# Converting the second network's weights during the first, storing them in DRAM, and reading its back-projection weights from there

## The chip, the cores and the metric

One core of a Trainium2 chip. The metric is device time of one launch in microseconds. The kernel before took 1028.5 us in the median of three runs (1026.12 to 1029.22).

## The reference, cut to what matters

The weights of both networks are float64 and reach the chip as such. Attention runs first (a full softmax over means of four rows, plus a local softmax over a band of seven positions); its output is x, 2304 tokens by 512. Two networks follow:

```
h = x @ w_in                 # 512 -> 2048
x = (h * cos(h)) @ w_out     # 2048 -> 512
a = x @ w_a                  # 512 -> 1536
b = x @ w_b
y = (a * b) @ w_out2         # 1536 -> 512
```

## The kernel before, in words

**Precision.** Each float32 operand of a matmul is split into a high part (rounded by a copy to fp32r on ACT) and a low part (a subtraction); a product is three matmuls, high times high, high times low and low times high (`mm3`, L417 to L421). A float64 weight of 128 x 512 arrives as pairs of 32-bit words (512 KB, tile `raw`) and is converted to float32 by one ACT instruction (L104) and two DVE instructions (L105, L106): this is one *conversion*.

**First network.** Tokens are cut into units of 288 (five) and 432 (two). A step g does one block of 128 hidden columns: `h_mm` (12 matmuls), cosine on ACT and DVE (`cos_a`, `cos_b`, L457 to L466), split into gh and gl (L470, L474), and three steps later `back_mm` (12 matmuls) into four accumulators. There are 112 steps; units 0 and 1 are done in two halves of 8 blocks each, so that their first half goes to `y_part` in DRAM and the second to `y_dram`. The attention of later units is dealt out over the steps by `unit_slots`, up to step 96. The 32 weight tiles of this network, as high and low parts, stay in SBUF in the pool `wp` (33 slots of 4 KB per partition).

**Second network.** It works on three groups G of 768 tokens, as a 2 x 2 block product with seven multiplications in place of eight (P1 to P7, over sums and differences of weight blocks and of x blocks). For each of six column blocks p and for a and b there are seven products (`product`, 6 matmuls each), written out by hand in the list `items` with the back-projection blocks (`back2`, 6 matmuls each) between them. Each group ends with a run of 24 back-projection blocks (its half h = 1) without products between. `load_x` fetches x from DRAM (and adds `y_part` on POOL for the tokens that have one, L630), `prep_x` forms the differences and splits seven x blocks (`xsplit`, L642, L643); both are done for the next group during that run, on DVE.

**Weights of the second network.** `take2` converts its 36 raw tiles and forms the sums of weight blocks on POOL (L593 to L596). It is called in the last 16 steps of the first network and during the products of the first group. `stage` (L717 to L726) then makes, a few items ahead, the high and low part of each weight block that an item needs, products and back-projection alike: a copy on ACT (L724) and a subtraction on POOL, every third on DVE (L726). Each group does this anew.

**Order.** A list scheduler sets the order on each engine from the program's order, the dependencies and the tiles' slots; each engine and SP's DMA queue then work strictly in that order. `after` adds an edge to this scheduling without a wait on the chip. SP issues all DMAs.

Of the kernel before, what the change touches and what calls it, by code (L numbers as in the profile page):

```python
# [9 lines left out]
F32 = mybir.dt.float32  # L10
# [13 lines left out]
KC = DM // 128  # L24
# [17 lines left out]
C = {'AHEAD': 8, 'LEAD': 4, 'NPRE': 4, 'ND': 'ddd', 'XL': 'dpp', 'SUMS0': 'dddd', 'SUMS1': 'pppp', 'GLO': 8, 'FS': 8, 'S1': 0.7, 'G2': 14, 'LC': 0, 'DM': 2, 'LAG': 3, 'NGS': 3, 'MK': 0, 'SB': 'ddd', 'NL': 'dpp', 'W0': 0, 'W1': 0, 'W2': 0, 'W3': 0, 'NWV': 3, 'NGH': 4, 'XB': 8, 'YE': 6, 'CA': 2, 'CV': 1.3, 'SA': 5, 'SD': 3, 'PA': 1, 'LAG2': 2, 'PK': 1.0, 'GE': 'ad', 'NXF': 3, 'LP': 0, 'T': {'sums': [0, 0.5, 1.0, 3.0], 'ls': [0, 0, 0, 1.5], 'ds': [1, 1.5, 3, 4], 'ex': 6, 'ln': [6.0, 9.5], 'dn': [6, 7, 9, 10], 'dt': [7, 9.5, 11, 12], 'lt': [7.5, 8.5, 12.0, 13.5], 'at': [9.5, 9.5, 13.5, 14.5], 'xh': [11.0, 12.0, 15.0, 15.5], 'xl': [12.5, 13.5, 15.5, 15.5]}, 'T1': {'sums': [0, 0, 1.0, 2.0], 'ls': [0.5, 1.5, 2.5, 3.5], 'ds': [1, 1.5, 3, 4], 'ex': 5, 'ln': [5.5, 8], 'dn': [5.0, 6.0, 8.0, 9.0], 'dt': [6.0, 7.5, 10.0, 11.0], 'lt': [7.0, 8.0, 12.0, 12.0], 'at': [9, 9, 13, 14], 'xh': [9.0, 10.0, 13.0, 14.0], 'xl': [9.5, 11, 15, 15]}}  # L42
# [16 lines left out]
def kernel(ctx, tc, qT, kT, vw, vds, w_in, w_out, w_a, w_b, w_out2, out):  # L59
# [42 lines left out]
    def to_f32(raw, out=None):  # L102
        lw, hh = raw[:, :, 0], raw[:, :, 1]
        act.activation(out=hh.bitcast(F32), in_=hh.bitcast(F32), func=AF.Prelu, scale=2.0 ** -112, alpha=2.0 ** 32)  # L104
        dve.tensor_scalar(out=lw, in0=lw, scalar1=29, scalar2=None, op0=ALU.logical_shift_right)  # L105
# [90 lines left out]
    def local_scores(u, hp):  # L196
# [21 lines left out]
        mx = at.tile([128, NW], F32, tag="mx", name="mx", bufs=3)  # L218
# [21 lines left out]
    def exps(u):  # L240
# [5 lines left out]
        for hp in range(HP if u < C["DM"] else 0):  # L246
            sm = smd[u, hp]
            sdr[u, hp] = at.tile([QD, 2], F32, tag="sd", name="sd", bufs=3)
# [247 lines left out]
    if True:  # L496
# [61 lines left out]
        order2 = [(nm, p + NP * i) for p in range(NP) for nm in "ab2" for i in range(2)]  # L558
        raw2, w1, w2, ssl = {}, {}, {}, {}
        cv = [0, 0]  # L560

        def fetch2(upto):
            while cv[0] < min(upto, len(order2)):
                nm, f = order2[cv[0]]
                raw2[nm, f], _ = wload(srcs[nm][f])
                cv[0] += 1

        def sblock(nm, p, k):
# [3 lines left out]
            return ssl[b // 4][:, b % 4]  # L572

        def take2(upto):
            while cv[1] < min(upto, len(order2)):
                nm, f = order2[cv[1]]
                i, p = divmod(f, NP)
                dst = w2 if nm == "2" else w1
                if (nm, p) == ("2", NP - 1):
                    fetch2(cv[1] + (3 if cv[1] < 30 else 2))  # L580
                    r = raw2.pop((nm, f))
                    to_f32(r)
                    w2[nm, p, i] = r[:, :, 0].bitcast(F32)
                    cv[1] += 1
                    continue
                if i == 0:
                    dst[nm, p] = wp.tile([128, 4, 256], F32, tag="w", name="w1", bufs=33)
# [285 lines left out]
```

## Time and profile before

| | us |
|---|---|
| profiled execution | 1030.88 |
| its span | 1029.1 |
| PE busy | 968.1 (94%) |
| DVE busy | 748.9 (73%) |
| ACT busy | 592.1 (58%) |
| POOL busy | 398.6 (39%) |

The busy share of PE in 40 equal slices of the span, each digit a tenth (9 is 90% or more), with that of DVE below:

```profile
PE   5978899999999899999979899999799999999998
DVE  7889966685757465663598998877877778686773
```

A slice is 25.7 us. The first network's steps end near 600 us, the groups of the second end near 742, 886 and 1026 us. Matmuls are pipelined, so that the busy time of PE is no measure of its pace; the number of matmuls in a stretch is.

### The profile page before, as it was taken

The page shows a single profiled execution, that of the slowest core. Times are in us where ns is not written, and L with a number is a line of the kernel's source. Part 1 is how long each engine was busy: PE and PEld are TensorE (multiplying, and loading weights), DVE is VectorE, ACT ScalarE, POOL GpSimd, SP SyncE. Part 2 cuts the span into 40 slices and gives each one's busy share as a digit, 9 for nine tenths or more (in the row PEclk, how much of TensorE's full clock was granted, in tenths as well). Part 3 has the DMA queues.
Part 4 walks back from the last instruction along what each step waited for, and adds up shares of the span by engine and source line. Part 5 has one row for each costly group of instructions (what it writes and reads, how often), then busy time and mean ns, then how long its engine had stood idle before and what let it go on. Part 6 is the DMA issues. An engine that isn't in the chain of part 4 may idle for free. (4 is left out here: it accounts for less than half of the span.)

```text
span 1029.1 us, 18838 instructions
## 1 busy us (share of the span) xinstructions
PE 968.1 (94%) x6936; PEld 920.2 (89%) x6936; DVE 748.9 (73%) x1524; ACT 592.1 (58%) x1390; POOL 398.6 (39%) x499
## 2 busy tenths in 40 slices
PE   5978899999999899999979899999799999999998
PEld 4767789999999799899878799999799999999998
DVE  7889966685757465663598998877877778686773
ACT  4677666474757456565656654545544446544453
POOL 4878731002100300000174484446644444544452
PEclk9989899999999999999999999999899999999999
DMA  9645421211120210000463640002200002000000
GB/s 301 216 160 205 123 73 38 77 48 55 58 69 20 82 31 27 29 2 1 119 223 123 235 149 1 1 1 86 76 9 1 2 1 93 32 1 1 2 32 31
DMA packets 35035, 72.84 MB, mean 71 GB/s; under 512 B 3968, under 2 KB 19840, under 8 KB 34944
## 3 DMA queue, kind: packets, MB, share of 16 engines
q1 hardware_dynamic: 34944, 71.65, 21.7%
q8 instruction: 55, 0.90, 0.4%
q14 instruction: 36, 0.29, 0.1%
HBM read 61.01 MB, written 10.62 MB: 70 GB/s over the span
## 5 line engine op out<-in xcount | busy, mean ns | idle before, releaser
L726 POOL TENSOR_TENSOR sb<-w,sb 128x256 fp32r<-128x256 f32 x183 | 144.4, 791 | 265.7 <-ACT sb L724 241.9
L744 DVE TENSOR_TENSOR ev<-ev,z 128x384 f32<-128x384 f32 x252 | 134.9, 549 | 56.4 <-PE z L420 50.3
L724 ACT ACTIVATE sb<-w 128x256 fp32r<-128x256 f32 x264 | 109.2, 416 | 95.7 <-PE z L420 70.3
L418 PE MATMUL h<-xh,w 128*128 128x288 f32 (+1 forms) x448 | 147.4, 329 | 13.8 <-DVE gs L466 13.6
L418 PE MATMUL acc<-gh,w 128*128 128x288 f32 (+1 forms) x448 | 147.5, 329 | 6.1 <-DVE ev L451 4.2
L419 PE MATMUL acc<-gl,w 128*128 128x288 f32 (+1 forms) x448 | 144.0, 321 | 3.9 <-DVE gl L474 2.2
L420 PE MATMUL h<-xh,w 128*128 128x288 f32 (+1 forms) x448 | 143.0, 319 | 1.4 <-POOL w L114 1.4
L419 PE MATMUL h<-xl,w 128*128 128x288 f32 (+1 forms) x448 | 143.8, 321 | 0.0
L420 PE MATMUL acc<-gh,w 128*128 128x288 f32 (+1 forms) x448 | 142.2, 317 | 0.0
L419 PE MATMUL acc<-gl,sb 128*128 128x384 f32 x288 | 99.1, 344 | 8.0 <-DVE gl L732 8.0
L418 PEld LDWEIGHTS h<-xh,w 128*128 128x128 f32 x448 | 86.4, 193 | 20.8 <-DVE gs L466 17.8
L420 PE MATMUL acc<-gh,sb 128*128 128x384 f32 x288 | 98.7, 343 | 0.0
L418 PE MATMUL acc<-gh,sb 128*128 128x384 f32 x288 | 98.6, 342 | 0.0
L418 PEld LDWEIGHTS acc<-gh,w 128*128 128x128 f32 x448 | 85.9, 192 | 13.7 <-DVE ev L451 5.2
L418 PE MATMUL z<-xh,sb 128*128 128x384 f32 x288 | 97.3, 338 | 0.5 <-DVE ev L744 0.5
L419 PE MATMUL z<-xl,sb 128*128 128x384 f32 x288 | 97.1, 337 | 0.0
L420 PE MATMUL z<-xh,sb 128*128 128x384 f32 x288 | 97.0, 337 | 0.0
L419 PEld LDWEIGHTS acc<-gl,w 128*128 128x128 f32 x448 | 85.9, 192 | 6.9 <-DVE gl L474 2.7
L420 PEld LDWEIGHTS h<-xh,w 128*128 128x128 f32 x448 | 86.8, 194 | 3.0 <-POOL w L114 1.7
L419 PEld LDWEIGHTS h<-xl,w 128*128 128x128 f32 x448 | 86.8, 194 | 1.5 <-issue 0.6
L420 PEld LDWEIGHTS acc<-gh,w 128*128 128x128 f32 x448 | 85.9, 192 | 1.5 <-issue 0.4
L457 ACT ACTIVATE gs<-h 128x288 int32<-128x288 f32 (+1 forms) x112 | 49.4, 441 | 62.8 <-PE h L420 62.5
(134 smaller groups left out, 2321.1 us busy)
## 6 DMA issues: line engine op xcount, KB each, us to landing
raw<-in_w_out_dram SPq DMA_DIRECT2D x28, 512.0 KB
raw<-in_w_in_dram SPq DMA_DIRECT2D x16, 512.0 KB
raw<-in_w_a_dram SPq DMA_DIRECT2D x12, 512.0 KB
raw<-in_w_b_dram SPq DMA_DIRECT2D x12, 512.0 KB
v<-in_vw_dram SPq DMA_DIRECT2D x16, 320.0 KB
q<-in_qT_dram SPq DMA_DIRECT2D x32, 146.0 KB
k<-in_kT_dram SPq DMA_DIRECT2D x16, 288.0 KB
vs<-in_vds_dram SPq DMA_DIRECT2D x32, 144.0 KB
```

Of the source, the lines that this page charges most:

```text
L418: i = pe.matmul(ps_out, lh, rh, start=start, stop=False)
L419: pe.matmul(ps_out, lh, rl, start=False, stop=False)
L420: pe.matmul(ps_out, ll, rh, start=False, stop=stop)
L457: act.activation(out=k, in_=hps[g], func=AF.Copy, scale=1.0 / (2.0 * math.pi))
L724: act.activation(out=t[:, 0], in_=blk, func=AF.Copy)
L726: (dve if nst[0] % C["SD"] == 0 else pool).tensor_tensor(out=t[:, 1], in0=blk, in1=t[:, 0].bitcast(F32), op=ALU.subtract)
L744: dve.tensor_tensor(out=dst, in0=a, in1=z, op=ALU.add)
```

## The change

- The 36 raw tiles of the second network are converted during the first. Conversion n has three stages, load, convert and store, each called at a step: the first 26 at steps 34 to 95, one per 2.3 steps; the other 10 at one per step, from step 97. Loads, stores and the first two instructions of a conversion are ordered behind that step's matmuls with `after`. For w_a and w_b the four sums follow on POOL, on pieces of 128 columns (the host lays these weights out anew); for w_out2 the high and low part are made. The result goes to DRAM (`wd`). Every second of the 26 uses a tile `praw` in the attention's pool, the others the one free slot of `wp`. For its room, mx and sd have two buffers in place of three, and up shares qd's.
- `fetch2` reads the w_a and w_b blocks and their sums back, from the fourth of the last 16 steps on and during the first 11 products.
- Back-projection blocks are no longer staged. `fetch_back` reads high and low part of one w_out2 tile (512 KB) for each group, half and block, 72 times, up to five ahead.
- `y_part` is added to `y_dram` during the first group's products, in eight pieces (`fold`): two loads, an addition on POOL and a store.
- `prep_x` is cut into pieces that are called one per back-projection block (three per step in the first network). In the run, gh and gl are made two uses ahead from its start; x is loaded one block earlier.
- Constants: CV 1.3 to 1.0, SA 5 to 6, new NE 26, RA 5.

```diff
-        mx = at.tile([128, NW], F32, tag="mx", name="mx", bufs=3)
+        mx = at.tile([128, NW], F32, tag="mx", name="mx", bufs=2)
...
-        up = at.tile([128, QD], F32, tag="up", name="up", bufs=1)
+        up = at.tile([128, QD], F32, tag="qd", name="up", bufs=2)
...
+        pre = [(nm, p, j) for p in range(NP) for nm in "ab2" for j in range(2)]
+        praw, wd, w1, ssl = {}, {}, {}, {}
+        NEARLY = C["NE"]
+        for p in range(NP):
+            for nm in "ab":
+                wd[nm, p] = dram.tile([128, 7, 256], F32, name=f"wd_{nm}{p}", tag=f"wd_{nm}{p}")
+            for f in (p, p + NP):
+                wd["2", f] = dram.tile([128, 2, 512], F32, name=f"wd_2{f}", tag=f"wd_2{f}")
+        pre_at = {}
+        for n in range(len(pre)):
+            if n < NEARLY:
+                t0 = 2 * NF + 2 + n * (NG - 3 * NF - 2 - 4.5) / (NEARLY - 1)
+            else:
+                t0 = NG - NF + 1 + (n - NEARLY)
+            for stage_, dt in enumerate((0, 2.4, 3.4) if n < NEARLY else (0, 2, 3)):
+                pre_at.setdefault(int(t0 + dt), []).append((stage_, n))
+
+        def pre_load(n, g):
+            nm, p, j = pre[n]
+            if n % 2 and n < NEARLY:
+                t = at.tile([128, 512, 2], U32, tag="praw", name="praw", bufs=1)
+            else:
+                t = wp.tile([128, 512, 2], U32, tag="w", name="praw", bufs=33)
+            ins = sp.dma_start(out=t.rearrange("p f e -> p (f e)").bitcast(I64), in_=srcs[nm][p + NP * j if nm == "2" else 2 * p + j])
+            after(ins, h_ins[g])
...
+        def pre_conv(n, g):
+            nm, p, j = pre[n]
+            t = praw[n]
+            hh = t[:, :, 1]
+            flat = t.rearrange("p f e -> p (f e)")
+            fb = flat.bitcast(F32)
+            k = len(marks)
+            to_f32(t, flat[:, :512], h_ins[g])
+            if nm == "2":
+                act.activation(out=flat[:, 512:].bitcast(F32R), in_=fb[:, :512], func=AF.Copy)
+                pool.tensor_tensor(out=flat[:, :512].bitcast(F32R), in0=fb[:, :512], in1=fb[:, 512:], op=ALU.subtract)
+            else:
+                a11, a12, a21, a22, s1, s2, s4 = (fb[:, 128 * i:128 * i + 128] for i in range(7))
+                pool.tensor_tensor(out=s1, in0=a21, in1=a22, op=ALU.add)
+                pool.tensor_tensor(out=s2, in0=s1, in1=a11, op=ALU.subtract)
+                pool.tensor_tensor(out=a21, in0=a11, in1=a21, op=ALU.subtract)
+                pool.tensor_tensor(out=s4, in0=a12, in1=s2, op=ALU.subtract)
+
+        def pre_store(n, g):
+            nm, p, j = pre[n]
+            flat = praw.pop(n).rearrange("p f e -> p (f e)")
+            if nm == "2":
+                ins = sp.dma_start(out=wd["2", p + NP * j].rearrange("p a b -> p (a b)"), in_=flat.bitcast(F32))
+            else:
+                ins = sp.dma_start(out=wd[nm, p][:, :, 128 * j:128 * j + 128],
+                                   in_=flat.bitcast(F32)[:, :896].rearrange("p (b c) -> p b c", c=128))
+            after(ins, h_ins[g])
+
+        order2 = [(kind, nm, p) for p in range(NP) for kind, nm in (("w", "a"), ("s", "a"), ("w", "b"), ("s", "b"))]
+        cv = [0]
...
+        def fetch2(upto):
+            while cv[0] < min(upto, len(order2)):
+                kind, nm, p = order2[cv[0]]
+                if kind == "w":
+                    t = w1[nm, p] = wp.tile([128, 4, 256], F32, tag="w", name="w1", bufs=33)
+                    sp.dma_start(out=t, in_=wd[nm, p][:, :4])
+                else:
+                    k = 0
+                    while k < 3:
+                        t, b = sblock(nm, p, k)
+                        n = min(3 - k, 4 - b)
+                        sp.dma_start(out=t[:, b:b + n], in_=wd[nm, p][:, 4 + k:4 + k + n])
+                        k += n
+                cv[0] += 1
...
-                n = min(N2, 2 * NB - s0)
-                yps = []
-                for k in range(2):
-                    if n > 0:
-                        yps.append(tile_of())
-                        sp.dma_start(out=yps[k][:, :n], in_=y_part[:, 2 * k + j, s0:s0 + n])
                 for k in range(2):
                     t = xb[k, h, j] = tile_of()
                     sp.dma_start(out=t, in_=y_dram[:, 2 * k + j, s0:s0 + N2])
-                    if n > 0:
-                        pool.tensor_tensor(out=t[:, :n], in0=t[:, :n], in1=yps[k][:, :n], op=ALU.add)
...
+        steps = []
+
+        def advance(n):
+            while n and steps:
+                try:
+                    next(steps[0])
+                    n -= 1
+                except StopIteration:
+                    steps.pop(0)
...
-                fetch2(2)
-                take2(int(max(0, i - 1) * C["CV"]))
+                fetch2(int(max(0, i - 2) * C["CV"]))
                 if i in (4, 6):
                     load_x(0, (i - 4) // 2, g2t)
-                if i in (8, 12):
-                    prep_x((i - 8) // 4, pool, g2t)
+                if i in (6, 9):
+                    steps.append(prep_x((i - 6) // 3, pool, g2t))
+                advance(3)
+            for stage_, n in pre_at.get(g, []):
+                (pre_load, pre_conv, pre_store)[stage_](n, g)
+            if g == NG - 1:
+                advance(100)
...
-            if it[0] == "prod":
-                blk = wblock(it[3], it[2], it[4])
-            else:
-                blk = w2["2", it[3]][:, 2 * it[4] + it[5]] if it[3] < NP - 1 else w2["2", it[3], it[4]][:, 256 * it[5]:256 * it[5] + 256]
+            if it[0] != "prod":
+                return
+            blk = wblock(it[3], it[2], it[4])
...
+        uses = [(G, h, p + NP * i) for G in range(len(GROUPS)) for h in range(2) for p in range(NP) for i in range(2)]
+        wring, wpos = {}, [0]
+
+        def fetch_back(upto):
+            while wpos[0] < min(upto, len(uses)):
+                u = uses[wpos[0]]
+                wring[u] = wp.tile([128, 2, 512], F32, tag="w", name="wb", bufs=33)
+                sp.dma_start(out=wring[u], in_=wd["2", u[2]])
+                wpos[0] += 1
+
+        def fold(m, h, stage_, hold={}):
+            if stage_ == 0:
+                hold[m, h] = t, yp = [p2.tile([128, NB], F32, tag="g2", name="yf", bufs=12) for _ in range(2)]
+                sp.dma_start(out=t, in_=y_dram[:, m, NB * h:NB * h + NB])
+                sp.dma_start(out=yp, in_=y_part[:, m, NB * h:NB * h + NB])
+            else:
+                t, yp = hold.pop((m, h))
+                ins = pool.tensor_tensor(out=t, in0=t, in1=yp, op=ALU.add)
+                after(ins, zlast[0])
+                sp.dma_start(out=y_dram[:, m, NB * h:NB * h + NB], in_=t)
+
+        zlast = [None]
...
-            sb = sbs.pop(k)
+            wb = wring[G, h, f]
+            if mh == 0:
+                fetch_back(uses.index((G, h, f)) + 1 + C["RA"])
+            else:
+                wring.pop((G, h, f))
...
+                mm3(acc[2 * mh + m], wb[:, 1, ms].bitcast(F32R), wb[:, 0, ms].bitcast(F32R), gh[G, h, f], gl[G, h, f], first, last)
...
+        fetch_back(2)
+        folds = [(m, h) for h in range(2) for m in range(KC)]
+        np_ = [0]
         AH = C["SA"]
         for k in range(AH):
             stage(k)
@@ -802,21 +890,29 @@
             stage(k + AH)
             if it[0] == "prod":
                 product(k, *it[1:])
-                if it[1] == 0 and it[4] in ("P6", "P4"):
-                    take2(cv[1] + 1)
+                if it[1] == 0:
+                    fetch2(cv[0] + 1)
+                    a, b = divmod(np_[0] - 4, 7)
+                    if 0 <= a < len(folds) and b in (0, 5):
+                        fold(*folds[a], b // 5)
+                    np_[0] += 1
...
-                if h == 1 and mh == 0:
-                    for r in ((0, 1, 2) if q == 0 else (q + 2,)):
-                        if r < NF2:
-                            f = r // 2 + NP * (r % 2)
-                            split_g((G, 1, f), g2.pop(f))
-                    if G + 1 < len(GROUPS):
-                        if q in (1, 5):
-                            load_x(G + 1, (q - 1) // 4, ev)
-                        if q in (3, 7):
-                            prep_x((q - 3) // 4, dve, ev)
+                if mh == 0 and (h == 1 or p == NP - 1):
+                    r = q + 2 if h == 1 else i
+                    if r < NF2:
+                        f = r // 2 + NP * (r % 2)
+                        split_g((G, 1, f), g2.pop(f))
+                    if h == 1 and G + 1 < len(GROUPS):
+                        if q in (0, 4):
+                            load_x(G + 1, q // 4, ev)
+                        if q in (2, 6):
+                            steps.append(prep_x((q - 2) // 4, dve, ev))
+                        if q == 11:
+                            advance(100)
+                if h == 1:
+                    advance(1)
```

## Rows read from the trace of the kernel before

**Rows 1.** Busy us (count) of PE, PEld, DVE, ACT, POOL; clock, DMA, GB/s

```profile
510.00:597.00 87.00, 74.67 (x356) 68.96 (x355) 76.39 (x116) 52.98 (x105) 51.31 (x53) 0.94 0.62 205
597.00:708.00 111.00, 110.10 (x628) 109.14 (x627) 90.89 (x169) 56.25 (x135) 60.82 (x78) 1.00 0.08 25
708.00:746.00 38.00, 31.80 (x165) 31.16 (x164) 31.32 (x45) 22.12 (x55) 24.16 (x27) 0.91 0.33 99
746.00:850.00 104.00, 104.00 (x595) 104.00 (x595) 77.18 (x145) 50.69 (x122) 48.72 (x66) 1.00 0.01 3
850.00:886.00 36.00, 34.16 (x188) 33.85 (x187) 29.86 (x55) 24.07 (x61) 19.47 (x21) 0.95 0.21 66
```

**Rows 2.** PE's waits, 440 to 1030 us: total us, times, longest

```profile
PE acc L419 <- DVE gl L732: 8.0, 3, 3.4
PE h L418 <- DVE gs L466: 6.5, 2, 4.7
```

**Rows 3.** Timeline of PE (start, duration), last unit

```profile
520.61 0.36 PE L418 MATMUL h<-xh,w 128*128 128x432 f32 x1
...
530.00 0.36 PE L418 MATMUL h<-xh,w 128*128 128x432 f32 x1
...
540.04 0.56 PE L419 MATMUL h<-xl,w 128*128 128x432 f32 x1
540.40 0.56 PE L420 MATMUL h<-xh,w 128*128 128x432 f32 x1
```

**Rows 4.** Groups, 510 to 597 us (busy us, mean ns | idle before)

```profile
L106 DVE SCALAR_TENSOR_TENSOR w<-raw 128x512 uint32<-128x512 uint32 x29 | 25.4, 881 | 1.3 <-ACT raw L104 0.4
L418 PE MATMUL acc<-gh,w 128*128 128x432 f32 x64 | 23.8, 372 | 3.6 <-ACT gh L470 1.8 <-DVE ev L451 1.8
L418 PE MATMUL h<-xh,w 128*128 128x432 f32 x51 | 19.5, 382 | 6.6 <-DVE gs L466 6.5
L105 DVE TENSOR_SCALAR raw<-raw 128x512 uint32<-128x512 uint32 x28 | 17.0, 611 | 2.2 <-DMA raw<-in_w_a_dram 1.2 <-DMA raw<-in_w_out_dram 0.6 <-DMA raw<-in_w_b_dram 0.2
```

**Rows 5.** Busy time of the engines, 209 to 490 us

```profile
209.00:490.00 281.00, 276.45 (x2510) 255.89 (x2510) 174.75 (x454) 167.79 (x390) 22.73 (x48) 0.99 0.13 38
```

**Rows 6.** Groups of DVE, 708 to 746 us

```profile
L732 DVE TENSOR_TENSOR gl<-g,gh 128x384 fp32r<-128x384 f32 x10 | 8.3, 834 | 1.3 <-ACT gh L730 1.3
L643 DVE TENSOR_TENSOR xl<-ev,xh 128x384 fp32r<-128x384 f32 x8 | 7.7, 983 | 0.2 <-ACT xh L642 0.2
```

**Rows 7.** A group of DVE, 746 to 850 us

```profile
L732 DVE TENSOR_TENSOR gl<-ev,gh 128x384 fp32r<-128x384 f32 x11 | 6.5, 593 | 0.8
```

**Rows 8.** Groups of the whole kernel: staging

```profile
L726 POOL TENSOR_TENSOR sb<-w,sb 128x256 fp32r<-128x256 f32 x183 | 144.4, 791 | 265.7 <-ACT sb L724 241.9 <-DVE ev L744 19.6 <-DVE ev L657 1.7
L724 ACT ACTIVATE sb<-w 128x256 fp32r<-128x256 f32 x264 | 109.2, 416 | 95.7 <-PE z L420 70.3 <-PE acc L420 23.1 <-issue 1.3
```

**Rows 9.** Timeline of SP's queue behind 337 us

```profile
337.24 9.21 SPq L160 DMA_DIRECT2D vs<-in_vds_dram  x3
346.54 0.35 SPq L452 DMA_DIRECT2D y_dram<-ev  x1
```

**Rows 10.** Timeline of PE behind 354 us

```profile
354.64 0.80 PE L205 MATMUL att<-k,q 64*64 64x64 f32 x20 [2.13 <-DVE xf L336]
358.18 1.33 PE L205 MATMUL att<-k,q 64*64 64x64 f32 x20 [2.41 <-DVE smx L216]
```

**Rows 11.** Busy time, 86 to 88 us (last number: GB/s)

```profile
86.00:88.00 2.00, 0.93 (x8) 0.70 (x6) 2.00 (x2) 1.80 (x4) 1.89 (x2) 1.00 1.03 419
```

**Rows 12.** Timeline, 497 to 502 us: a load and its reader

```profile
497.65 0.33 SPq L100 DMA_DIRECT2D raw<-in_w_a_dram  x1
501.44 0.43 DVE L105 TENSOR_SCALAR raw<-raw 128x512 uint32<-128x512 uint32 x1 [0.79 <-DMA raw<-in_w_a_dram]
```

**Rows 13.** PE's waits, 0 to 120 us

```profile
PE att L307 <- DVE smd L291: 2.5, 1, 2.5
```

**Rows 14.** Timeline of SP's queue behind 860 us

```profile
860.37 9.05 SPq L628 DMA_DIRECT2D ev<-y_dram  x6
```

More of the change, by code (lines that the diff above doesn't have):

```diff
@@ L100, in wload, with to_f32 @@
         return t, sp.dma_start(out=t.rearrange("p f e -> p (f e)").bitcast(I64), in_=src)
-    def to_f32(raw, out=None):
+    def to_f32(raw, out=None, behind=None):
         lw, hh = raw[:, :, 0], raw[:, :, 1]
-        act.activation(out=hh.bitcast(F32), in_=hh.bitcast(F32), func=AF.Prelu, scale=2.0 ** -112, alpha=2.0 ** 32)
-        dve.tensor_scalar(out=lw, in0=lw, scalar1=29, scalar2=None, op0=ALU.logical_shift_right)
+        ins = act.activation(out=hh.bitcast(F32), in_=hh.bitcast(F32), func=AF.Prelu, scale=2.0 ** -112, alpha=2.0 ** 32)
+        after(ins, behind)
+        ins = dve.tensor_scalar(out=lw, in0=lw, scalar1=29, scalar2=None, op0=ALU.logical_shift_right)
+        after(ins, behind)
         ins = dve.scalar_tensor_tensor(out=lw if out is None else out, in0=hh, scalar=3, in1=lw, op0=ALU.logical_shift_left, op1=ALU.bitwise_or)
@@ L247, in exps @@
             sm = smd[u, hp]
-            sdr[u, hp] = at.tile([QD, 2], F32, tag="sd", name="sd", bufs=3)
+            sdr[u, hp] = at.tile([QD, 2], F32, tag="sd", name="sd", bufs=2)
             for a in range(2):
@@ L264, in down_exp @@
         sm = smd[u, hp]
-        sdr[u, hp] = at.tile([QD, 2], F32, tag="sd", name="sd", bufs=3)
+        sdr[u, hp] = at.tile([QD, 2], F32, tag="sd", name="sd", bufs=2)
         for a in range(2):
@@ L280, in down_norm @@
         if u >= C["DM"]:
-            s = at.tile([QD, 2], F32, tag="sd", name="sd", bufs=3)
+            s = at.tile([QD, 2], F32, tag="sd", name="sd", bufs=2)
             dve.tensor_reduce(out=s, in_=sm, axis=AX.X, op=ALU.add)
@@ L571, in sblock @@
                 ssl[b // 4] = wp.tile([128, 4, 256], F32, tag="w", name="ws", bufs=33)
[L572 to L587, printed above, removed]
-                t = dst[nm, p]
-                fetch2(cv[1] + (3 if cv[1] < 30 else 2))
-                to_f32(raw2.pop((nm, f)), t[:, 2 * i:2 * i + 2].rearrange("p a b -> p (a b)").bitcast(U32))
-                if i == 1 and nm != "2":
-                    s1, s2, s4 = (sblock(nm, p, k) for k in range(3))
-                    pool.tensor_tensor(out=s1, in0=t[:, 2], in1=t[:, 3], op=ALU.add)
-                    pool.tensor_tensor(out=s2, in0=s1, in1=t[:, 0], op=ALU.subtract)
-                    pool.tensor_tensor(out=t[:, 2], in0=t[:, 0], in1=t[:, 2], op=ALU.subtract)
-                    pool.tensor_tensor(out=s4, in0=t[:, 1], in1=s2, op=ALU.subtract)
-                cv[1] += 1
+            return ssl[b // 4], b % 4
+        def fetch2(upto):
[12 more added lines that the diff above has]
+                cv[0] += 1
         def wblock(nm, p, what):
@@ L739, in product @@
                 js = slice(128 * j, 128 * j + 128)
-                mm3(z, sb[:, 0, js], sb[:, 1, js], *xt[rhs[what], j], j == 0, j == 1)
+                ins = mm3(z, sb[:, 0, js], sb[:, 1, js], *xt[rhs[what], j], j == 0, j == 1)
+            zlast[0] = ins.ins
             c = cs.setdefault(nm, {})
@@ L785, in back2 @@
                     acc[2 * mh + m] = ps.tile([128, N2], F32, tag=f"acc{2 * mh + m}", name="acc")
-                ms = slice(128 * m, 128 * m + 128)
-                mm3(acc[2 * mh + m], sb[:, 0, ms], sb[:, 1, ms], gh[G, h, f], gl[G, h, f], first, last)
+                ms = slice(256 * mh + 128 * m, 256 * mh + 128 * m + 128)
+                mm3(acc[2 * mh + m], wb[:, 1, ms].bitcast(F32R), wb[:, 0, ms].bitcast(F32R), gh[G, h, f], gl[G, h, f], first, last)
             if last:
@@ L834, in cols, with blocks @@
         return w.reshape(KC, 128, n, 128).transpose(2, 1, 0, 3).reshape(n, 128, KC * 128)
+    def blocks(w):
+        return w.reshape(2, 2, 128, 2, NP, 128).transpose(4, 1, 2, 3, 0, 5).reshape(2 * NP, 128, 512)
     vw = np.empty((NU, HP // 2, 2, W, NW, 2, D), v.dtype)
@@ L846, in _layout @@
         "w_in": cols(moe_w_in), "w_out": moe_w_out.reshape(NF, 128, DM),
[L847 removed]
+        "w_a": blocks(moe2_w_a), "w_b": blocks(moe2_w_b), "w_out2": moe2_w_out.reshape(NF2, 128, DM),
     }
```

27 lines of the change are left out of this document (15 added, 12 removed).

## The prediction

> **What bounds the kernel now.** I read the 40 slices of the page first: PE's digit is 9 from slice 6 on, except in slices 14, 21, 23 and 29 and the last. Those places were then cut out with the view of busy time by stretches [rows 1], and PE's waits in them were listed [rows 2]. The reader should see that PE is the bound almost everywhere behind 200 us, so that a change there can only win what PE still loses, and that the loss sits in three places.
>
> The loss is counted as matmuls times the spacing they have when nothing stops them. For 384 columns that is 104.0 / 595 = 0.1748 us, from the stretch 746 to 850, which is busy throughout [rows 1]. For 432 columns, 48 matmuls lie between the starts at 520.61 and 530.00, so 0.1956 us [rows 3]. The stretch 510 to 597 holds 64 x 3 + 51 x 3 = 345 matmuls of 432 columns [rows 4], and 356 - 345 = 11 of 384: 67.5 + 1.9 = 69.4 us of work in 87, a loss of 17.6. In the same way 597 to 708 loses 111 - 628 x 0.1748 = 1.2, 708 to 746 loses 38 - 28.8 = 9.2, and 850 to 886 loses 36 - 32.9 = 3.1. Together 31.1 us.
>
> Not all of it is waiting. After the wait of 4.7 us on gs [rows 2] the 432-column matmuls start 0.36 apart (540.04, 540.40) [rows 3] and not 0.1956: PE came back at the lower of its two clocks, 1.2 of 2.4 GHz; over 510 to 597 the granted clock is 0.94, over 708 to 746 0.91 [rows 1]. A stall that goes takes this tail with it, which is why I count matmuls and not waits.
>
> What PE waits for is DVE: gs and gl of the loops [rows 2]. In 510 to 597 DVE is busy 76.39 of 87 us, in 708 to 746 31.32 of 38 [rows 1].
>
> **Part 1: the conversions leave the last unit.** In 510 to 597 there are 29 conversions at 0.881 (L106) and 0.611 us (L105) [rows 4], 43 of DVE's 76 us. In the new kernel 26 of the 36 are tied to steps 34 to 95, one per 2.3 steps, and 10 to steps 97 to 109. So 19 of the 29 go, 19 x 1.49 = 28.3 us, and DVE is left with 48 us beside 69 of PE work, 69%; before 500 us it held PE nearly always at a similar share [rows 5]. The x preparation is also dealt out three pieces a step instead of in one block. I leave one wait of the shorter kind there, 6.5 - 4.7 = 1.8 [rows 2], plus 0.7 of slow clock: 2.5 instead of 17.6, a gain of 15.1 (bounds 0, if the rest still bunches up, and 17.6). Behind it, at 597 to 708, conversions and sums are gone too: 1.2 becomes 0.7, gain 0.5.
>
> **Part 2: the turn from one token group to the next.** At 708 to 746 DVE runs x preparation, gl and a third of the staging subtractions, while POOL does the y_part additions and the other staging. Its operations with two SBUF inputs take 834 (gl, L732) and 983 ns (xl, L643) [rows 6]; gl took 593 in the calmer stretch behind it [rows 7]. In the new kernel the 144 staged back-projection blocks of the 396 staged ones disappear, each 0.416 us of ACT and about 0.79 of POOL or a DVE slot [rows 8]; the y_part additions are done during the first group's products; gl is issued two uses ahead; and the preparation goes one piece per block. What is left for DVE in some 25 us of back-projection is 12 gl, 14 xl and 8 differences, 34 x 0.593 = 20 us at the calm price [rows 7]. That fits, though not by much. 9.2 becomes 1.2 (gain 8.0, bounds 4 and 9.2). At 850 to 886, where y_part plays no part, 3.1 becomes 0.8 (gain 2.3, bounds 0 and 3.1). PE itself is late next: nothing is won below its spacing.
>
> The folding itself costs 16 loads, 8 additions and 8 stores, in a stretch where POOL is busy 60.82 of 111 us [rows 1] and loses a third of its staging. Hidden; without that cover, PE would still not wait for it, since its results are read tens of us later.
>
> **Part 3: what the 26 early conversions cost between 209 and 490 us.** DVE is busy 174.75 of 281 us there, ACT 167.79, POOL 22.73 [rows 5]. At 1.49 the conversions add 39 us to DVE: 76%. ACT gets under 30 us, POOL under 60. No engine becomes the bound. The queues are the danger: each conversion puts a load and a store on SP, and the store waits there until POOL (or ACT and DVE before it) has finished, with the q, k, v, vs and y loads and stores behind it. The trace has a precedent. Three vs loads held SP for 9.21 us from 337.24, and the y store came only at 346.54 [rows 9]. Its tile was not free, DVE waited, and PE stood still 2.13 and 2.41 us [rows 10], 4.5 together. Bounds: -4.5, if the new order dissolves this one, and +18, if the other four attention stretches of steps 32 to 96 each get one. Most loads are issued steps ahead, so I take +2.5, about one collision in two chances.
>
> **Part 4: back-projection weights from DRAM.** 72 fetches of 512 KB. A use is 12 matmuls, 12 x 0.1748 = 2.1 us. In the runs of back-projection alone (12 uses, three times) the fetches need 524 KB / 2.1 us = 250 GB/s; the DMA engines moved 419 GB/s from 86 to 88 us [rows 11], so a queued fetch takes 1.25 us. A lone 512 KB load was issued at 497.65 and let DVE go at 501.44, 3.8 us later [rows 12]. The fetch is issued five uses ahead, 10.5 us. Of the 33 slots 12 hold w1, 9 ws and 5 xw; 7 are left for 6 fetches in flight, so the slot asked for was left two uses before. I take +0.7 for all 72 (bounds 0 and rival C).
>
> The Trainium skill ("DMA: Bandwidth & Descriptors", "Anatomy of one DMA") fits a transfer at 2.0 us plus its bytes over 436 GB/s, for another way of issuing: an estimate of 3.2 us for 512 KB. Taken one after the other this would be more than a use lasts, and 36 uses would wait 1.1 us each: about 40 us, 1046 in all. Nothing above rests on it; the row at 419 GB/s shows that queued transfers overlap that fixed part.
>
> **Part 5: smaller buffers** (mx, sd 3 to 2, up shares qd). sd can hold back an exponential until the norm two heads before is done; the nearest row is a wait for a norm in the opening, 2.5 us [rows 13]. Bounds -2.5 and +2.5 (the order on the engines changes); I take 0.
>
> **The sum.** 15.1 + 0.5 + 8.0 + 2.3 = 25.9 won, 2.5 + 0.7 lost: 22.7. The profiled execution took 1030.88 us (span 1029.1), so 1008.2 of its kind; it was 2.4 above the median of 1028.5, against which the forecast stands: 1028.5 - 22.7 = 1005.8, called 1006.
>
> **Rivals.**
>
> B. Collisions on SP in the middle. For it: the precedent [rows 9, 10], and 52 more transfers on the queue that caused it. Against: PE stood still only once in 281 us there, and loads have steps of slack. With two more collisions, 9 + some 1.5 of slow clock in place of 2.5: 1014; with four, 1022.
>
> C. Slower: the back weights come late. SP is held by an x load that waits for its tile; six of them held it 9.05 us from 860.37, in just such a run [rows 14]. The reserve is 10.5 - 3.8 = 6.7 us, so one hold of that kind costs PE some 2.4 us; if it recurs, or if the slots are not free, so that a fetch starts only with the use before, each use waits 3.8 - 2.1 = 1.7 us: 36 x 1.7 = 61, 1067. It decides the sign from 22.7 / 36 = 0.63 us of wait per use. Against: the bandwidth [rows 11], and that the x loads start earlier in the run and the x work no longer blocks their tiles in one lump.
>
> D. The change doesn't do what it says: the ten late conversions, the preparation and the evacuation still meet in the last unit, and half of the 17.6 stays. 8.8 in place of 2.5: 1012.
>
> **How the numbers follow.** Forecast 0.62 (its own range 996 to 1011), B 0.20, D 0.10, C 0.08. Low end: 1028.5 - 31.1 = 997 with no cost at all, and 995 with the present stall at 354 us half gone. High end 1019: most of B and all of D; left out are C, the worst of B and what lies below 995, about 0.17. About 0.3% can be told from no change. Faster by more: 0.62 + 0.10 + 0.18 of B = 0.90. Within: 0.02 of B and 0.02 of C. Slower: 0.06, all C.
>
> **What would show it.** Right: the stretch of the last unit about 15 us shorter with DVE near 70%; no PE wait on gl in the turns; no wait of PE on a DMA of wb; the middle at most 5 us longer. Wrong: PE waiting for wb in the three runs (C), for smx, xf or a q load between 210 and 500 us (B), or for gs behind step 96 (D).

## The result, and the profile after

The changed kernel takes 1012.22 us (median of 4 runs, 1010.78 to 1013.94), the kernel before, beside it, 1027.43 (1026.12 to 1029.22): ratio 0.9851 [0.9827, 0.9876], 15.2 us won where 22.7 were forecast. The profiled execution took 1010.78 us (span 1009.0), 20.1 less than that of before.

Line numbers shift by two between the kernels: the three matmuls of `mm3`, L418 to L420 before, are L420 to L422 in the kernel after. From its page: PE and DVE in 40 slices, busy times, the chain of waits by engine.

```profile
PE   5878799999899999999998999999999999999998
DVE  7788976587577877766466657676677667676751
PE 960.7 (95%) x6936; PEld 915.4 (91%) x6936; DVE 704.1 (70%) x1476; ACT 546.0 (54%) x1258; POOL 344.5 (34%) x463
PE 80%; DVE 6%; POOL 5%; DMA 4%; ACT 2%; issue 1%; SPq 1%; POOLq 0%; ACTq 0%; DVEq 0%
```

Behind slice 22 PE's digit is 9 to the last but one, where before it fell in slices 23 and 29, and the chain that ended last runs over PE for 80% of the span. The digit now falls to 8 in slice 11 (252 to 277 us) and slice 22 (530 to 555). Why slice 11 is new is told below.

The stretches were cut anew at anchors that both kernels have: the first h matmul of the last unit's step 96, the first products of groups 1, 2 and 3, the last matmul. Busy time by stretches of the kernel after, columns as in [rows 1], the first four lines answering to [rows 1], the last to [rows 5]:

```profile
501.53:588.78 87.25, 84.06 (x421) 80.20 (x420) 54.43 (x89) 53.41 (x106) 33.40 (x42) 0.98 0.78 270
588.78:727.09 138.31, 138.31 (x793) 138.28 (x792) 97.53 (x186) 59.12 (x139) 50.57 (x64) 1.00 0.47 157
727.09:865.73 138.64, 138.64 (x793) 138.64 (x793) 96.88 (x186) 59.27 (x139) 42.91 (x56) 1.00 0.36 118
865.73:1004.21 138.48, 138.48 (x792) 138.48 (x792) 85.55 (x162) 49.98 (x117) 37.84 (x50) 1.00 0.25 80
209.00:490.00 281.00, 275.42 (x2477) 254.11 (x2475) 204.42 (x511) 184.81 (x424) 72.73 (x128) 0.99 0.42 131
```

The same stretches of the kernel before, at the same anchors:

```profile
495.11:595.19 100.08, 87.75 (x422) 81.45 (x420) 83.65 (x128) 61.42 (x122) 51.30 (x54) 0.95 0.57 186
595.19:744.44 149.25, 142.14 (x794) 140.55 (x792) 123.35 (x215) 78.99 (x191) 84.99 (x104) 0.98 0.15 45
744.44:887.01 142.57, 140.74 (x793) 140.42 (x793) 108.23 (x202) 76.03 (x186) 69.23 (x88) 0.99 0.07 21
887.01:1025.46 138.45, 138.45 (x792) 138.45 (x792) 95.08 (x178) 68.53 (x166) 63.45 (x84) 1.00 0.04 12
```

The reader is to see that a group of the second network now takes 138.3 to 138.6 us three times over, which is 793 x 0.1748 = 138.6: nothing is left to win there. PE's only wait behind 510 us is `gs` in the last unit (it answers to [rows 2]); none is on `wb`. PE's waits, 510 to 1010 us, then 130 to 510:

```profile
PE h L420 <- DVE gs L468: 3.2, 1, 3.2
```
```profile
PE att L207 <- ACT praw L596: 3.8, 1, 3.8
PE acc L420 <- DVE ev L453: 3.3, 3, 1.9
```

The wait at L207 for `praw` is new. With every profiled run cut at the start of certain steps' first h matmul (us; worked out from PE's timeline; z is the first product of the second network, and group 3 ends with the start of the last matmul), it can be placed:

```
              0-34   44-48  64-72   96-z   group 1  group 2  group 3
before       204.71  18.90  42.25  100.08  149.25   142.57   138.45
after        208.91  25.21  38.18   87.25  138.31   138.64   138.48
after again  210.07  25.45  37.61   87.99  138.32   138.64   138.48
e1           216.14  18.90  41.98   98.99  149.95   142.19   138.45
e2           207.29  25.88  38.41   85.75  138.29   138.64   138.48
e3           209.93  27.30  41.42   86.46  138.37   138.64   138.48
e4           212.50  18.90  42.48   93.80  183.22   138.64   138.48
e5           212.39  24.66  37.93   86.43  138.32   139.26   138.48
e6           209.88  24.10  37.79   89.93  138.30   138.64   138.48
e7           213.51  24.64  38.00   88.55  149.85   150.12   145.71
e7b          208.80  25.32  37.42   87.91  139.47   141.03   138.45
e8           210.35  25.75  37.80   87.20
e9           204.48  18.91  36.77   89.49  138.31   138.64   138.47
e10          205.85  26.00  38.30   88.01  138.31   138.64   138.48
```

(In e8 the groups overlap: products of the next one start within the run before.) After less before: +4.2 to step 34, where no conversion runs yet; +6.3 and -4.1 in two places of the middle, while the steps between agree to 0.1; -12.8 in the last unit; -14.9 in groups 1 and 2; and +1.2 behind the last matmul. Where nothing was changed, the groups repeat to 0.1 us from run to run. Steps 64 to 72 repeat to 1 us, steps 44 to 48 to 2; the last unit and the opening scatter by 4 to 5. The profiled execution of before lay 3.5 us above its median and that of after 1.4 below, which is why 20.1 us stand beside 15.2.

### The profile page after: what moved, and what is told of

Read it like the earlier page. It is cut to its first block, busy times and chain, and to the rows that moved or that the text cites. A ratio compares the mean times of both kernels' runs of the same rounds, so it can differ in the third digit from the quotient of the medians.

```text
span 1009.0 us, 18867 instructions
## 1 busy us (share of the span) xinstructions
PE 960.7 (95%) x6936; PEld 915.4 (91%) x6936; DVE 704.1 (70%) x1476; ACT 546.0 (54%) x1258; POOL 344.5 (34%) x463
## 4 chain that ended last, share of the span: by engine, by line
PE 80%; DVE 6%; POOL 5%; DMA 4%; ACT 2%; issue 1%; SPq 1%; POOLq 0%; ACTq 0%; DVEq 0%
PE acc L420 10%; PE acc L421 10%; PE acc L422 10%; PE z L421 9%; PE z L422 9%; PE z L420 9%; PE h L420 6%; PE h L421 5%; PE h L422 5%; DMA vs<-in_vds_dram 2%; PE att L326 2%; PE att L207 1%; DVE raw L108 1%; PE att L319 1%; PE att L234 1%
## 5 line engine op out<-in xcount | busy, mean ns | idle before, releaser
L420 PE MATMUL h<-xh,w 128*128 128x288 f32 (+1 forms) x448 | 147.6, 329 | 8.6 <-DVE gs L468 8.5
L420 PE MATMUL acc<-gh,w 128*128 128x288 f32 (+1 forms) x448 | 146.2, 326 | 3.9 <-DVE ev L453 3.9
L422 PE MATMUL h<-xh,w 128*128 128x288 f32 (+1 forms) x448 | 143.1, 319 | 2.2 <-POOL w L116 2.2
L422 PE MATMUL acc<-gh,w 128*128 128x288 f32 (+1 forms) x448 | 141.6, 316 | 0.0
L783 POOL TENSOR_TENSOR sb<-w,sb 128x256 fp32r<-128x256 f32 x96 | 76.1, 794 | 185.9 <-ACT sb L781 140.1
L420 PEld LDWEIGHTS h<-xh,w 128*128 128x128 f32 x448 | 86.5, 193 | 15.3 <-DVE gs L468 12.1
L420 PE MATMUL acc<-gh,wb 128*128 128x384 f32 x288 | 96.9, 337 | 0.0
L422 PE MATMUL acc<-gh,wb 128*128 128x384 f32 x288 | 96.9, 337 | 0.0
L422 PE MATMUL z<-xh,sb 128*128 128x384 f32 x288 | 96.9, 336 | 0.0
L420 PE MATMUL z<-xh,sb 128*128 128x384 f32 x288 | 96.9, 336 | 0.0
L421 PE MATMUL acc<-gl,wb 128*128 128x384 f32 x288 | 96.9, 336 | 0.0
L781 ACT ACTIVATE sb<-w 128x256 fp32r<-128x256 f32 x144 | 59.9, 417 | 66.2 <-PE z L422 63.1
L420 PEld LDWEIGHTS acc<-gh,w 128*128 128x128 f32 x448 | 85.1, 190 | 10.6 <-DVE ev L453 5.0
L783 POOL TENSOR_TENSOR sb<-ws,sb 128x256 fp32r<-128x256 f32 x72 | 54.5, 757 | 108.6 <-ACT sb L781 84.8
L422 PEld LDWEIGHTS h<-xh,w 128*128 128x128 f32 x448 | 86.6, 193 | 4.5 <-POOL w L116 2.4
L422 PEld LDWEIGHTS acc<-gh,w 128*128 128x128 f32 x448 | 85.3, 190 | 1.4 <-issue 0.4
```

The costliest lines, as they stand in the source:

```text
L420: i = pe.matmul(ps_out, lh, rh, start=start, stop=False)
L421: pe.matmul(ps_out, lh, rl, start=False, stop=False)
L422: pe.matmul(ps_out, ll, rh, start=False, stop=stop)
L781: act.activation(out=t[:, 0], in_=blk, func=AF.Copy)
L783: (dve if nst[0] % C["SD"] == 0 else pool).tensor_tensor(out=t[:, 1], in0=blk, in1=t[:, 0].bitcast(F32), op=ALU.subtract)
```

## The experiments

### Small buffers: e1, e2, e10

e1 is the kernel before with only the smaller buffers; e2 the kernel after with `mx` and `sd` back at 3; e10 with `sd` alone. The edit of e2 (e10 without its first two lines):

```diff
-        mx = at.tile([128, NW], F32, tag="mx", name="mx", bufs=2)
+        mx = at.tile([128, NW], F32, tag="mx", name="mx", bufs=3)
-            sdr[u, hp] = at.tile([QD, 2], F32, tag="sd", name="sd", bufs=2)
+            sdr[u, hp] = at.tile([QD, 2], F32, tag="sd", name="sd", bufs=3)
...
```

> The kernel before, with only the three smaller buffers of the change (mx and sd with two buffers, up in the buffers of qd). In the changed kernel, step 34 of the first network starts 4.2 us later than before (208.91 against 204.71), though nothing that the change adds has run by then. Theory S: the smaller buffers reorder and hold back the opening; then this kernel reaches step 34 at about 208 to 209 us and takes about 4 us more than before (1031 to 1032). Rival N: the 4.2 us are the scatter of single executions; then step 34 stays within 1 us of 204.7 and the time within 2 us of before.

> The changed kernel, with mx and sd back at three buffers (up still shares qd's, for there is no room). Theory S, if mx and sd are the cause: step 34 back at about 204.7 us and 4 us less than the changed kernel, about 1008. Rival: if sharing qd is the cause, step 34 stays at 209 and the time at 1012; the same if it is scatter.

> The changed kernel with sd alone back at three buffers. mx and sd together won 0.8% of the kernel before (0.977 against 0.985), some 8 us in the opening. Theory sd (an exponential on ACT waits for the norm two heads before): nearly all of it is sd, 0.977 to 0.979. Rival mx (the row maxima are what the third buffer frees): the ratio stays at 0.985.

e1 took 1040.02 us, 1.0064 [1.0039, 1.009] of the kernel before beside it: the buffers alone cost 0.4 to 0.9%. e2 took 1008.81, 0.9772 [0.9747, 0.9797]. e10, on another chip, 1008.0, 0.978 [0.9757, 0.9804], where the unchanged kernel after took 1012.67, 0.9824 [0.98, 0.9847]. So it is `sd`, at 4.7 us; giving `mx` its buffer back too brings nothing more that shows (0.9772 against 0.978). The table says where: nine profiled runs of the changed kernel with `sd` at 2 (after, after again, e3 to e8) reach step 34 at 208.8 to 213.5 us, mean 210.7, the three with 3 (e2, e9, e10) at 204.5 to 207.3, mean 205.9. The 4.8 us between them agree with the 4.7 of the medians. Which instruction is held there was not followed.

> The changed kernel itself, as the measure for the others on the same chip. Both theories: 0.985 of the kernel before, groups of 138.3 to 138.6 us, 25 us from step 44 to 48 (before 18.9); the start of step 34 scatters by some us from run to run.

### The middle: e3, e9

Between steps 44 and 48 of the kernel after, SP's queue (start, length, issue), then POOL, ACT and PE:

```profile
248.08 4.46 SPq L162 DMA_DIRECT2D vs<-in_vds_dram  x2
252.59 0.97 SPq L152 DMA_DIRECT2D v<-in_vw_dram  x1
253.66 0.38 SPq L583 DMA_DIRECT2D praw<-in_w_out_dram  x1
...
257.81 0.53 SPq L611 DMA_DIRECT2D wd_b<-praw  x1
258.39 1.65 SPq L143 DMA_DIRECT2D q<-in_qT_dram  x2
```
```profile
257.32 0.46 POOL L603 TENSOR_TENSOR praw<-praw 128x128 f32<-128x128 f32 x1
257.96 0.65 ACT L104 ACTIVATE praw<-praw 128x512 f32<-128x512 f32 x1 [4.87 <-DMA praw<-in_w_out_dram]
...
260.90 0.63 ACT L596 ACTIVATE praw<-praw 128x512 fp32r<-128x512 f32 x1
...
262.03 1.33 PE L207 MATMUL att<-k,q 64*64 64x64 f32 x20 [3.82 <-ACT praw L596]
```

The store of a conversion waited on SP for the sums of POOL (done at 257.78); the q loads behind it went out at 258.39, and by its semaphore the first of them had landed at 261.94, 0.1 us before PE went on. At the same time ACT, in its own order, stood 4.87 us for the next raw tile. Two theories: the store holds q on SP, or the conversion stands in ACT's order ahead of what PE needs. e3 lets the store be issued a step later:

```diff
-            for stage_, dt in enumerate((0, 2.4, 3.4) if n < NEARLY else (0, 2, 3)):
+            for stage_, dt in enumerate((0, 2.4, 4.4) if n < NEARLY else (0, 2, 3)):
```

> The changed kernel, with the store of the 26 early conversions called two steps after the conversion and not one. In the changed kernel PE loses 6.3 us between steps 44 and 48: a store to DRAM stands on SP's queue from 254.0 to 257.8 us, waiting for POOL's sums, and two q loads behind it are issued only at 258.4; PE stands still until 262.0. Theory Q (the q load behind the store is what PE waits for): the loss between steps 44 and 48 falls from 6.3 us to under 2, and the time by 4 to 6 us, unless the next load, which needs the tile that the store empties, holds the queue in the same way. Rival A (ACT, which waited 4.9 us for a raw tile in its order, is the cause): nothing changes there, since load and conversion stay where they are.

It took 1016.81 us, 0.9851 [0.9815, 0.9887], as the kernel after; the stretch took 27.3 us. The later store met the next group of loads. SP, ACT and PE of e3:

```profile
245.48 8.75 SPq L162 DMA_DIRECT2D vs<-in_vds_dram  x3
254.29 0.66 SPq L611 DMA_DIRECT2D wd_b<-praw  x1
...
258.47 0.35 SPq L583 DMA_DIRECT2D praw<-in_w_out_dram  x1
...
262.41 0.66 ACT L104 ACTIVATE praw<-praw 128x512 f32<-128x512 f32 x1 [8.14 <-DMA praw<-in_w_out_dram]
...
264.01 1.33 PE L207 MATMUL att<-k,q 64*64 64x64 f32 x20 [4.63 <-ACT smd L237]
```

Here q was not late; a raw load was, behind the vs loads and the store, ACT stood for it 8.14 us, and the attention's ACT work (L237) behind it released PE. So neither theory holds alone, and the old collision was mostly back too (steps 64 to 72: 41.42). What both have in common is a conversion at the dense attention of these steps, where SP's queue is held by the vs loads; the delay reaches PE by whatever stands behind it, a load or an engine. e9 therefore begins no conversion in steps 39 to 48 (by its formula, loads are called at 38 and next at 49; 22 early ones instead of 26, and the buffers of e2):

```diff
-                t0 = 2 * NF + 2 + n * (NG - 3 * NF - 2 - 4.5) / (NEARLY - 1)
+                t0 = 2 * NF + 2 + n * (NG - 3 * NF - 2 - 13.5) / (NEARLY - 1)
+                t0 += 9 * (t0 > 39)
...
-                t0 = NG - NF + 1 + (n - NEARLY)
+                t0 = NG - NF + 1 + (n - NEARLY) * 10 / 14
```

> The changed kernel with mx and sd at three buffers, 22 early conversions in place of 26, and none of them begun in the ten steps 41 to 50, in which the vs loads of an attention unit occupy SP's queue and POOL; 14 late ones, at 1.4 per step. Theory B (SP's queue, shared with conversions, is what costs 6.3 us at steps 44 to 48): this stretch falls from 25 us to 18.9, the last unit gets 1 to 3 us longer, and the time is 4 us or so below that with the larger buffers alone: ratio 0.973. Rival: the loss moves to the next unit with vs loads (steps 64 to 72, now 38.2 us), and the ratio stays at 0.977 or rises.

1002.04 us (1000.96 to 1004.38), 0.9724 [0.9701, 0.9748]; steps 44 to 48 took 18.91 us, as before the change. SP's queue there:

```profile
243.40 4.18 SPq L162 DMA_DIRECT2D vs<-in_vds_dram  x2
247.67 0.75 SPq L152 DMA_DIRECT2D v<-in_vw_dram  x1
248.51 10.19 SPq L143 DMA_DIRECT2D q<-in_qT_dram  x4
```

With no store or raw load among them, the q loads start 2.7 us behind step 44 (245.78 in this run) instead of 8.9 (249.45 in the kernel after), and SP's long hold on q (10.19 us) costs PE nothing. So conversions in these steps are shown to be the cause. That it is SP's queue, and not the work on ACT, DVE and POOL that left with them, is argued from the lines above; no run parts the two. The four conversions more in the last unit are no clear loss: 89.5 us, where the runs with ten late ones take 85.8 to 89.9. This version beats both kernels.

### When to convert: e4

All 36 conversions in the last unit again, ordered and stored as in the kernel after:

```diff
- 'NE': 26
+ 'NE': 0
-                t0 = NG - NF + 1 + (n - NEARLY)
+                t0 = NG - NF + 1 + n * 10 / 36
-                    fetch2(int(max(0, i - 2) * C["CV"]))
+                    fetch2(int(max(0, i - 6) * C["CV"]))
```

> The changed kernel, with all 36 conversions called in the last unit, at steps 97 to 109, and the reads of their results called four steps later for it. All other parts of the change stay. Theory D (the conversions on DVE were what the last unit lost its time to): from step 96 to the first product it takes again 98 to 102 us, as before (100.1), against 87.3 in the changed kernel, and the middle wins the 6 us that the early conversions cost it: about 1012 + 13 - 6 = 1019. Rival P (the spread x preparation is what relieved the last unit): it stays under 91 us, and the time falls below 1010.

1060.9 us, 1.0279 [1.0246, 1.0313]. The last unit took 93.8, 6.5 more than in the kernel after, about half of what had been won there. The edit puts back only part of the old load, though: DVE runs 24 conversions in the last unit, 30 in the kernel before, 10 in the kernel after; the other 12 come behind the first product. Steps 44 to 48 and 64 to 72 are as before the change (18.90, 42.48): both the new collision and the end of the old one come from the early conversions. The rest of the time is in group 1, 183.2 us. Busy time around its start, and PE's wait:

```profile
545.00:597.00 52.00, 45.70 (x217) 41.30 (x216) 36.60 (x60) 31.02 (x61) 33.29 (x45) 0.97 1.06 375
597.00:640.00 43.00, 9.03 (x27) 6.06 (x25) 26.78 (x35) 16.50 (x36) 34.42 (x46) 0.54 0.82 272
...
644.28 0.69 PE L420 MATMUL z<-xh,sb 128*128 128x384 f32 x1 [22.07 <-ACT ev L828]
```

The DMA engines are full (1.06, 375 GB/s) from 545 to 597 us with raw loads, stores and the reading back together; then PE runs 27 matmuls in 43 us at a granted clock of 0.54. With everything in the last unit the round trip through DRAM costs more than the change wins; tied to early steps it does not.

### The turns: e5, e6, e7, e7b

One part of the change is undone at a time. e5 lets the x preparation run as a block, e6 adds `y_part` at the turn as before, e7 stages the 144 back-projection blocks again without reading them, e7b stages blocks of w_a and lets PE read these in the back-projection instead of the fetched w_out2 (its output is therefore not the reference's).

```diff
e5
                     steps.append(prep_x((i - 6) // 3, pool, g2t))
+                    advance(100)
e6
+                    if n > 0:
+                        pool.tensor_tensor(out=t[:, :n], in0=t[:, :n], in1=yps[k][:, :n], op=ALU.add)
...
-        folds = [(m, h) for h in range(2) for m in range(KC)]
+        folds = []
e7, e7b
-            if it[0] != "prod":
-                return
-            blk = wblock(it[3], it[2], it[4])
+            blk = wblock(it[3], it[2], it[4]) if it[0] == "prod" else wblock("a", it[3], "P1")
e7b
-                mm3(acc[2 * mh + m], wb[:, 1, ms].bitcast(F32R), wb[:, 0, ms].bitcast(F32R),
+                mm3(acc[2 * mh + m], sb[:, 0, ms], sb[:, 1, ms],
...
```

> The changed kernel, with the x preparation called in one block again instead of piece by piece. In the changed kernel the stretch from step 96 to the first product takes 87.3 us (before 100.1), the group from its first product to the next group's first 138.3 (before 149.3 and 142.6). Theory L (the lump was a cause): the last unit takes 90 to 94 us, the two groups that prepare a next one 140 to 143 us. Rival S (staging and POOL's additions were the cause): both stay within 1 us of the changed kernel.

> The changed kernel, with y_part loaded and added at the turn to the second group again, as before the change. Theory Y: the first group, 138.3 us in the changed kernel, takes 140 to 144 us, since before the change this turn lost 9.2 us and the next one, without y_part, 3.1. Rival: with staging gone, POOL and DVE have room for the 8 additions, and it stays under 139.

> The changed kernel, with the staging work of the 144 back-projection blocks put back on ACT, POOL and DVE (from a block that is there; nobody reads the result). PE and the DMAs do the same as in the changed kernel. Theory S (staging loaded the engines in the runs): the first two groups take 140 us or more each. Rival: the lump or y_part was the cause, and they stay at 138.3 to 139.

> The changed kernel with back-projection blocks staged as before the change, high and low part on ACT, POOL and DVE a few items ahead, and read by PE, so that PE paces the staging; the blocks come from w_a and not from w_out2, so the output is not the reference's, and w_out2 is not fetched. Theory S (staging is what made the turns late): the first two groups take 141 to 146 us in place of 138.3 and 138.6. Rival (the other parts of the change, the spread preparation and the early y, would have been enough): both under 139.5.

e5 took 1012.57 us in its one run, with 0 and 0.6 us more in groups 1 and 2; e6 1012.37, with nothing; e7b 1013.18, with 1.2 and 2.4. None of these brings back the 10.9 of group 1, so each explanation by one of these parts fell there; staging alone is more than half of group 2's 3.9, and with it PE waits for gl again:

```profile
PE acc L421 <- DVE gl L810: 2.4, 3, 0.9
```

e7 took 1047.21, all three groups longer, and is no clean undoing: nobody reads its blocks, so PE does not pace them, and POOL makes 17 in a row while PE waits for the evacuation of `acc`.

```profile
697.04 15.29 POOL L781 TENSOR_TENSOR sb<-w,sb 128x256 fp32r<-128x256 f32 x17 [0.53 <-ACT sb L779]
```

The kernel after has a DVE with room. DVE at the first turn of the kernel after, 690 to 740 us, and of e7b, 690 to 732:

```profile
L812 DVE TENSOR_TENSOR gl<-g,gh 128x384 fp32r<-128x384 f32 x12 | 6.7, 562 | 4.2 <-ACT gh L810 4.2
L677 DVE TENSOR_TENSOR xl<-ev,xh 128x384 fp32r<-128x384 f32 x8 | 4.2, 552 | 0.0
```
```profile
L810 DVE TENSOR_TENSOR gl<-g,gh 128x384 fp32r<-128x384 f32 x12 | 8.9, 744 | 0.4 <-ACT gh L808 0.4
L677 DVE TENSOR_TENSOR xl<-ev,xh 128x384 fp32r<-128x384 f32 x8 | 6.3, 792 | 0.3 <-ACT xh L676 0.2
```

Against 834 and 983 ns in [rows 6], gl and xl cost 562 and 552; with staging put back, 744 and 792. In the kernel after, DVE idles 4.2 us ahead of gl, for ACT's gh: it is no longer behind. With staging 0.4 are left, and PE loses little; in e5 and e6 DVE still idles 1.6 and 4.7 us ahead of gl.

One part of the change was undone by no run: gl is issued two uses ahead. In the kernel before, PE stood at this turn for a gl that had the block of x preparation ahead of it in DVE's order, eight operations of it and one of staging between 721.16 and 727.67 (DVE, then PE):

```profile
720.69 0.55 DVE L732 TENSOR_TENSOR gl<-g,gh 128x384 fp32r<-128x384 f32 x1
...
725.40 2.35 DVE L643 TENSOR_TENSOR xl<-ev,xh 128x384 fp32r<-128x384 f32 x2
727.67 0.55 DVE L732 TENSOR_TENSOR gl<-g,gh 128x384 fp32r<-128x384 f32 x1
```
```profile
728.27 0.69 PE L419 MATMUL acc<-gl,sb 128*128 128x384 f32 x1 [3.36 <-DVE gl L732]
```

Two uses are 4.2 us of PE's work, so the earlier issue alone could hide such a wait, in e5 and e6 too. Whether the last 9.7 us of group 1 come from it, or from staging, `y_part` and the block together, stays open: no run took it back, and no run took back all three.

### Late back weights: e8

The fetches go through two tiles in turn, so that one can start only when the use before the last has ended:

```diff
- 'RA': 5
+ 'RA': 1
-                wring[u] = wp.tile([128, 2, 512], F32, tag="w", name="wb", bufs=33)
+                if wpos[0] < 2:
+                    wbt.append(wp.tile([128, 2, 512], F32, tag="w", name="wb", bufs=33))
+                wring[u] = wbt[wpos[0] % 2]
```

> The changed kernel, with the 72 fetches of back-projection weights through two fixed tiles in place of up to seven slots, so that a fetch can start only when the use before the last has ended, 2.1 us before it is needed. A lone 512 KB load took 3.8 us in the kernel before. Theory C (the reserve in time is what hides the fetch): each use in the three runs of 12 waits about 1.7 us, some 20 us a run, more with the slow clock; groups of 158 us and more, 60 us in all or more. Rival W (only the rate counts, and that is far below what the DMA engines move): under 5 us in all.

1059.19 us in its one run; from the first product to the last matmul 460.3 us in place of 415.4, +44.9. Most of it is waits for `wb`, and the granted clock fell to 0.95 from 849 to 916 us, where the second run lies. PE's waits:

```profile
PE acc L420 <- DMA wb<-wd: 26.6, 24, 3.6
```

So rival C is a real mechanism of the right sign, and 44.9 against its 61 the right order: in the last run a use took some 3.0 us, not 3.8. The fetch itself costs what [rows 12] said: one issued at 1030.13 was read from 1033.77 on, 3.6 us later. But it is issued when the use before the last has ended, so a tile's round is a fetch and a use, 3.6 + 2.4 = 6.0 us, and two tiles share it. The Trainium skill ("DMA: Bandwidth & Descriptors", "Anatomy of one DMA") fits a transfer, for another way of issuing, at an estimated 3.2 us for this size; the 3.6 here agree in size. The kernel after does not work like that: with five ahead, PE waits for `wb` not once.

## Why the prediction was right, and where not

**What bounds it** held: all that was won is PE's lost time, and the count of matmuls by their spacing gave the floor that groups 1 to 3 now stand on.

**Part 1** (forecast 15.1): 12.8. DVE is busy 54.43 of 87.25 us, 62%, where 48 us and 69% were forecast. The one wait that was left in the sum came, on `gs` as said, but 3.19 us long and not 1.8. Behind it the clock was the slow one (the matmuls at 547.95 and 548.31 start 0.36 us apart and not 0.1956). PE, and DVE before it:

```profile
547.15 0.47 PE L420 MATMUL h<-xh,w 128*128 128x432 f32 x1 [3.19 <-DVE gs L468]
...
547.95 0.56 PE L420 MATMUL h<-xh,w 128*128 128x432 f32 x1
548.31 0.56 PE L421 MATMUL h<-xl,w 128*128 128x432 f32 x1
```
```profile
543.66 1.52 DVE L677 TENSOR_TENSOR xl<-xb,xh 128x384 fp32r<-128x384 f32 x2 [0.95 <-ACT xh L676]
545.11 0.68 DVE L106 TENSOR_SCALAR praw<-praw 128x512 uint32<-128x512 uint32 x1
545.89 0.69 DVE L108 SCALAR_TENSOR_TENSOR praw<-praw 128x512 uint32<-128x512 uint32 x1
546.50 0.60 DVE L468 SCALAR_TENSOR_TENSOR gs<-gs,h 128x432 f32<-128x432 f32 x1
```

So x preparation and a late conversion stood ahead of gs in DVE's order: rival D's mechanism, on a smaller scale. The unit stands 5 us above 420 x 0.1956 = 82.2. e4 shows some 6.5 of the 12.8 as the conversions' own, with 14 of the 20 put back; the rest stays open, since the block preparation (e5) cost nothing there and the unit scatters by some 2 us either way.

**Part 2** (8.0 + 2.3, and 0.5 ahead of it: 10.8): 14.9. My remainders of 1.2, 0.8 and 0.7 us were too careful: nothing remains. The upper bounds were even passed by a little, 10.9 in group 1 against 1.2 + 9.2 = 10.4 and 3.9 in group 2 against 3.1, since my stretches had missed part of the loss. The price of DVE's work fell below the calm price of [rows 7] that I had used, 562 and 552 against 593 ns. That the lighter DVE is what won it is shown for 1.2 us of group 1 and 2.4 of group 2 (e7b); for the rest gl's earlier issue is a rival that no run excludes.

**Part 3** (-2.5): -2.2, by luck in its size. "One collision in two chances" were in fact both: a new one of 6.3 us at steps 44 to 48, and the end of the old one of [rows 9, 10], 4.1 of its 4.5 us. Rival B's mechanism is there, once, at about its price of 4.5 and some slow clock: a wait of 3.82 us, and a granted clock of 0.52 from 262 to 268 us. (For four more of them the prediction's 1022 should be 1024, by the price that it used for two.) DVE rose to 204.42 of 281 us, 73% (76 forecast), and bounded nothing.

**Part 4** (-0.7): 0; PE waited for no `wb`.

**Part 5** (0, bounds 2.5 either way): this is the term that was mis-sized. The smaller `sd` costs 4.7 us by the medians on one chip, up to 8 by e2 against the kernel after on different ones, and lies outside its bounds. The nearest row [rows 13] was one wait of 2.5 us on a norm; the runs showed 4.8 us in the mean to step 34, and which instructions lose it was not followed. Without it, the sum is met: e2 won 1032.46 - 1008.81 = 23.65 us, e10 1030.65 - 1008.0 = 22.65, against 22.7. So the total was missed by this one term. That the rest adds up so closely is luck in part: in the profile part 1 is off by -2.3 us, parts 2, 3 and 4 by +4.1, +0.3 and +0.7, and 1.2 us are lost behind the last matmul.

**Rivals.** D is refuted for the most part: not half of the 17.6 stayed (8.8) but 5 us, though its sign, a wait on gs behind step 96, came. So did B's, a wait for a q load between 210 and 500 us, once. C did not occur.

## What to carry to other kernels

Count the matmuls of a stretch times their undisturbed spacing before asking what waits: it says what can be won, slow clock included. Here a transfer added to an in-order issue queue cost nothing at most places and 6.3 us at the densest one, by what stood behind it, so cut the kernel by steps, find such a place, and leave it out of the schedule (e9 against e10: 6 us for a shift of a few steps and four conversions moved to the last unit). A buffer taken from a chain of small tiles is not free because one row shows one short wait; try it by itself.

## What was not expected of the hardware

PE held its spacing of 0.1748 us over a whole group with the DMA engines moving 157 GB/s beside it. DVE's operations with two SBUF inputs differ by more than half from kernel to kernel: the same xl took 983 ns in [rows 6], 792 in e7b and 552 in the kernel after. Between the last two stands the staging on ACT, POOL and DVE (and the fetch of `wb`, which e7b lacks); which of them slows DVE was not tried. And the releaser that a wait names can be one of several: the wait of 3.82 us is put down to ACT's L596, which ended at 261.53, while the first q load behind the store was issued only at 258.39 and landed at 261.94; PE went on at 262.03.
